# Remaining keys and remaining queries of an attention kernel on four 64x64 tiles of TensorE, in a new order of steps

## The chip, the cores and the metric

The kernel runs on one core of a Trainium2 chip. The metric is the device time of one execution in microseconds (us). Matrix products run on TensorE (PE in the profile; PEld is its loading of weights), the other work on VectorE (DVE), ScalarE (ACT) and GpSimd (POOL); SyncE (SP) issues most DMAs.

## The reference

Attention over 8 batches of 8 heads, 576 positions of 64 channels, with rotary positions on queries and keys, and then a layer of 8 experts of which each token takes its best one.

```python
def rotate(x):
    x1, x2 = (x[..., :half], x[..., half:])
    return np.concatenate([x1 * cos - x2 * sin, x1 * sin + x2 * cos], axis=-1)
q_rot, k_rot = (rotate(q), rotate(k))
scores = scale * np.matmul(q_rot, k_rot.transpose(0, 1, 3, 2))
scores = scores - np.max(scores, axis=-1, keepdims=True)
attn = np.exp(scores)
attn = attn / (np.sum(attn, axis=-1, keepdims=True) + 1e-09)
x = np.matmul(attn, v)            # heads side by side: 4608 tokens x 512
...
expert_idx = np.argmax(x @ w_gate, axis=1)
out = gate_w * (np.maximum(x @ w1[e], 0) @ w2[e])   # e: the token's expert
```

## The kernel before

Attention works on 32 pairs of heads, one pair in a window; the heads of a pair lie on partitions 0 to 63 and 64 to 127. The 576 positions are 512 "main" ones, in four tiles of 128, and 64 "remaining" ones. `PLAN` lists the steps of a window in order, each with its engine (the last letter: p PE, v DVE, a ACT, g POOL, d a DMA on SP's queue) and an offset: window w performs a step with offset -3 for pair w+3. Every engine keeps the order of this list, so an instruction that waits holds up all behind it on its engine. The steps that matter here:

- `FQ`, `FK` load queries and keys, each beside a copy with its two channel halves exchanged. `RQ`, `RK` (L394 to L396) rotate them on POOL: two products and a sum of 128x576 each, into `yq` and `yk`.
- `HQ`, `LQ`, `HK`, `LK` split the rotated values into a high and a low part for fp32r products. `DH`, `DL` are DMAs that copy `q` to the other half of the partitions. `cR` (L438, ACT) copies the remaining queries from `q` into `zq`, which holds zeros between them.
- `S0` to `S8` (L459) are the scores of 128 queries against 576 keys: three products (high by high, low by high, high by low) of 288 columns on each of two row tiles (rows 0 to 63 and 64 to 127), each row tile into a bank of its own. `S4` has the remaining queries of both heads and needs twice as many products, with the zeros of `zq` in the other head's columns. `M` (L470, DVE) takes the scores out of PSUM with their maximum; there are two buffers of scores. `E` (L477, ACT) is the exponential.
- `TA`, `TB`, `TR` (L494, L501, L505) transpose the weights of attention on PE, and `cA`, `cB`, `c1`, `c2`, `c3` (L411) copy them into `PT` (main keys) and `PR` (remaining keys of both heads, 64 partitions each).
- `V0` to `V9` (L534) multiply them with v in fp32, the heads on two column tiles of 64 columns each: five products of 288 columns for each half of the queries, four with main keys and one with the remaining keys, in which `vr` (128x128) holds zeros for the other head. `U` copies the result to `uT`.
- `O` (L555, ten products of 72 columns) turns it to tokens and multiplies with the gate's weights `iw`; `X` (L579, DVE) scales it into `xt`.

The lines named G1 to GS in the plan are places where the steps of the gate are put in: the gate's logits, its choice (`oh`, L143), ranks, stores of tokens, and lists of tokens by indirect DMA from POOL (L694). From the fourth window before the last, the routing (`f1g`, `f1p` and others) comes in small DVE steps behind the steps of `RSTEP`. After the last windows the experts' layer runs over tokens in slots of 256 (L942, L974), its weights split by ACT and DVE (L880, L881); the last pair's `V`, `U`, `O` and `X` are merged with its first products.

A matmul of fp32 data stands in the trace as two matmul instructions, each with its own weight load; one of fp32r as one.

Of the kernel before, what the change touches and what calls it, by code (L numbers as in the profile page):

```python
# [41 lines left out]
STORES = (
    [("gS0d", 3, "GS"), ("gS1d", 4, "GS"), ("gS2d", 5, "GS"), ("gS4d", 5, "ZDd"), ("gS3d", 6, "GS")],
    [("gS0d", 3, "FQd"), ("gS1d", 3, "FKd"), ("gS2d", 3, "DHd"), ("gS3d", 3, "GS"), ("gS4d", 3, "VPd")],
# [33 lines left out]
def kernel(  # L78
# [17 lines left out]
    HS = S // 2  # L96
    XW = D + E
# [338 lines left out]
    def do_cR(st, n):  # L436

        nc.scalar.copy(out=zq[n % 2][:, :, 1:5:2].rearrange("p l a d -> p a l d"), in_=st["q"][:, :, :, 512:576].bitcast(F32))  # L438

    def do_S(st, n, j):  # L440
# [5 lines left out]
        todo = []  # L446
        for hc in (0, 1) if j == 4 else (h,):
            for qp, kp in ((0, 0), (1, 0), (0, 1)):
                todo.append((hc, qp, kp))
        for i_, (hc, qp, kp) in enumerate(todo):  # L450
            for u in range(2):
                r = slice(64 * u, 64 * u + 64)
                other = int(hc != u)
                if j == 4:
                    a = 1 + 2 * other - hc
                    lhs = zq[n % 2][r, qp, a:a + 2].rearrange("p a b -> p (a b)")
                else:
                    lhs = st["q"][r, other, qp, i * P:(i + 1) * P]
                nc.tensor.matmul(sp[:, u, 0:HS], lhsT=lhs, rhs=st["k"][r, kp, hc], start=(i_ == 0), stop=(i_ == len(todo) - 1))  # L459

# [13 lines left out]
    def do_E(st, n, j):  # L474
# [32 lines left out]
    def pt_tiles(st):  # L507
        if "PT" not in st:
            st["PT"] = pp.tile([P, 2, 4, S], F32, name="PT")
            st["PR_"] = pp.tile([P, S], F32, name="PR")  # L510

    def do_c(st, n, h, u, eng):
        pt_tiles(st)
        tp = st.pop(("T", h, u))
        copy(eng, st["PT"][:, h, 2 * u:2 * u + 2, 0:512].rearrange("p k (i b q) -> p b k i q", i=4, b=2),
             tp.rearrange("p b (k i q) -> p b k i q", k=2, i=4))

    def do_c1(st, n, eng):
        pt_tiles(st)
        copy(eng, st["PT"][:, :, :, 512:576], st["TR"][:, :, 0:256].rearrange("p h (k q) -> p h k q", k=4))  # L520

    def do_c2(st, n, eng):
        copy(eng, st["PR_"][:, 0:512].rearrange("p (i b q) -> p b i q", i=4, b=2),
             st["TR"][:, :, 256:512].rearrange("p b (i q) -> p b i q", i=4))

    def do_V(st, n, s):

        half, kt = divmod(s, 5)
        if s == 0:
            st["av"] = tp_tile()  # L530
        hs = slice(half * HS, half * HS + HS)
        for h in range(2):
            r = slice(h * 64, h * 64 + 64)
            nc.tensor.matmul(  # L534
                st["av"][r, half, 0:HS], lhsT=st["vn"][:, h, kt, :] if kt < 4 else vr[n % NVR][:, r],
                rhs=st["PT"][:, h, kt, hs] if kt < 4 else st["PR_"][:, hs], start=(kt == 0), stop=(kt == 4))
# [9 lines left out]
    AHEAD = 2  # L546
    late = []

    def do_O(st, n):

        o = st["O"] = tp_tile()
        for c in range(5 if n >= 0 else 0):
            for h in range(2):
                r = slice(64 * h, 64 * h + 64)
                nc.tensor.matmul(o[:, h, c * XW:c * XW + XW], lhsT=uT[r, c * P:c * P + P], rhs=iw[r, n % NP, :], start=True, stop=True)  # L555
# [633 lines left out]
```

## Time and profile before

| | us |
|---|---|
| median of 3 runs | 965.54 |
| lowest and highest | 962.71, 966.04 |
| the profiled execution, its own time | 964.9 |
| its span, first to last instruction | 963.1 |
| PE busy | 924.5 |
| ACT busy | 678.7 |
| DVE busy | 674.5 |
| POOL busy | 493.8 |

Busy times are means over two stages with different limits: windows of attention up to about 465 us of the span, and the experts' layer behind them.

### The profile page before, as it was taken

How to read it: one execution, taken by the hardware profiler on the slowest of the kernel's cores; microseconds unless marked ns; L12 is line 12 of the kernel's file. 1: busy time of each engine (PE TensorE's matmuls, PEld its weight loads, DVE VectorE, ACT ScalarE, POOL GpSimd, SP SyncE). 2: the span in 40 equal slices, each digit the busy share in tenths (PEclk: the TensorE clock that was granted, in tenths of full speed). 3: DMA queues.
4: the chain of work that ended last, by engine and by line, in shares of the span. 5: the costliest groups of instructions: out<-in, count | busy, mean ns of one | idle time of the engine just before them, and what ended most of it. 6: DMA issues, size and time to landing. Idle time of an engine off the chain costs nothing.

```text
span 963.1 us, 25337 instructions
## 1 busy us (share of the span) xinstructions
PE 924.5 (96%) x9720; PEld 797.8 (83%) x9720; DVE 674.5 (70%) x1354; ACT 678.7 (70%) x1217; POOL 493.8 (51%) x401
## 2 busy tenths in 40 slices
PE   6689999999999999999899999999999999999997
PEld 5578788877788878877698999999999999987886
DVE  5557787878787787886577666666666666667987
ACT  3699999999899999988444455445545545547875
POOL 6888789999899998980424122222222111110111
PEclk7689999999999999999999999999999999999999
DMA  7556666566565666545421377424415311155991
GB/s 256 152 167 186 198 186 204 156 193 196 169 191 159 195 195 190 153 121 156 153 69 47 127 232 234 142 63 153 134 60 184 98 47 47 45 188 190 369 341 51
DMA packets 93139, 153.98 MB, mean 160 GB/s; under 512 B 23127, under 2 KB 56599, under 8 KB 91984
## 3 DMA queue, kind: packets, MB, share of 16 engines
q1 hardware_dynamic: 84720, 129.88, 44.5%
q0 software_dynamic: 8000, 21.20, 6.5%
q8 instruction: 79, 1.29, 0.6%
q10 hardware_dynamic: 288, 1.18, 0.4%
q14 instruction: 52, 0.43, 0.1%
HBM read 162.47 MB, written 23.80 MB: 193 GB/s over the span
## 4 chain that ended last, share of the span: by engine, by line
PE 76%; issue 9%; DMA 5%; POOL 4%; ACT 3%; DVE 2%; another core or an unknown queue 0%; POOLq 0%; SPq 0%; ACTq 0%; DVEq 0%
PE hp L942 18%; PE yp L974 17%; PE tp L534 15%; PE sp L459 13%; PE tp L494 6%; PE tp L555 3%; DMA out_dram<-y,gi 3%; DMA qk<-in_qk_dram 2%; PE xps L897 1%; ACT pn L477 1%; ACT PT L411 1%; PE tp L505 1%; POOL qk L395 1%; PE tp L501 1%; POOL out_dram L984 1%
## 5 line engine op out<-in xcount | busy, mean ns | idle before, releaser
L470 DVE TENSOR_SCALAR_CACHE_REDUCE pn<-sp 128x576 f32<-128x576 f32 x256 | 190.9, 753 | 42.8 <-PE sp L459 39.1
L477 ACT ACTIVATE pn<-pn,negm 128x576 f32<-128x576 f32 x256 | 196.9, 773 | 1.6 <-DVE pn L470 1.6
L459 PE MATMUL sp<-k,q 64*128 64x288 f32 x1536 | 156.3, 322 | 15.9 <-DMA q<-q 8.6
L411 ACT COPY PT<-tp 128x1024 f32<-128x1024 f32 (+1 forms) x160 | 146.1, 929 | 26.7 <-PE tp L494 22.8
L942 PE MATMUL hp<-xh,w1h 128*128 128x256 f32 x544 | 154.3, 284 | 0.7 <-issue 0.4
L942 PE MATMUL hp<-xl,w1h 128*128 128x256 f32 x544 | 154.1, 283 | 0.0
L942 PE MATMUL hp<-xh,w1l 128*128 128x256 f32 x544 | 154.0, 283 | 0.0
L459 PEld LDWEIGHTS sp<-k,q 64*128 64x128 f32 x1536 | 116.0, 195 | 33.8 <-issue 20.8
L984 POOL DMA_INDIRECT out_dram<-y,gi x34 | 34.3, 1008 | 204.4 <-DVE y L147 181.0
L881 DVE TENSOR_TENSOR w2l<-r,w2h 128x1024 fp32r<-128x1024 f32 x92 | 111.6, 1230 | 36.3 <-ACT w2h L880 32.0
L534 PE MATMUL tp<-PT,vn 128*64 128x288 f32 x1024 | 136.7, 409 | 0.0
L974 PE MATMUL yp<-w2h,hh 128*128 128x512 f32 x320 | 126.8, 396 | 0.0
L974 PE MATMUL yp<-w2h,hl 128*128 128x512 f32 x320 | 124.8, 390 | 0.0
L974 PE MATMUL yp<-w2l,hh 128*128 128x512 f32 x320 | 124.6, 389 | 0.0
L881 DVE TENSOR_TENSOR w1l<-r,w1h 128x1024 fp32r<-128x1024 f32 x96 | 113.1, 1218 | 5.4 <-ACT w1h L880 4.4
L534 PEld LDWEIGHTS tp<-PT,vn 128*64 128x64 f32 x1024 | 70.7, 137 | 49.2 <-ACT pn L477 2.6
L942 PEld LDWEIGHTS hp<-xh,w1h 128*128 128x128 f32 x544 | 104.3, 192 | 2.1 <-DVE lpi L140 0.6
L910 ACT ACTIVATE hh<-hp 128x512 fp32r<-128x512 f32 x68 | 40.6, 597 | 91.7 <-PE hp L942 88.4
L942 PEld LDWEIGHTS hp<-xh,w1l 128*128 128x128 f32 x544 | 104.3, 192 | 0.7
L942 PEld LDWEIGHTS hp<-xl,w1h 128*128 128x128 f32 x544 | 104.3, 192 | 0.4 <-issue 0.4
L880 ACT CAST w2h<-r 128x1024 fp32r<-128x1024 f32 x92 | 94.9, 1043 | 11.2 <-PE tp L555 8.3
L880 ACT CAST w1h<-r 128x1024 fp32r<-128x1024 f32 x96 | 95.7, 1051 | 0.0
(194 smaller groups left out, 1805.9 us busy)
## 6 DMA issues: line engine op xcount, KB each, us to landing
r<-in_moe_w_dram SPq DMA_DIRECT2D x192, 512.0 KB
qk<-in_qk_dram SPq DMA_DIRECT2D x64, 576.0 KB
q<-q SPq DMA_DIRECT2D x128, 144.0 KB
x_dram<-xt SPq DMA_DIRECT2D x32, 288.0 KB
vn<-in_v_dram SPq DMA_DIRECT2D x32, 256.0 KB
xlist<-mark SPq DMA_DIRECT2D x8, 289.0 KB
x_dram<-xt SPq DMA_DIRECT2D x8, 144.0 KB
vr<-in_v_dram SPq DMA_DIRECT2D x64, 16.0 KB
```

Source lines behind the costliest of these rows:

```text
L411: (nc.scalar.copy if eng == "a" else nc.vector.tensor_copy)(out=o, in_=i)
L459: nc.tensor.matmul(sp[:, u, 0:HS], lhsT=lhs, rhs=st["k"][r, kp, hc], start=(i_ == 0), stop=(i_ == len(todo) - 1))
L470: nc.vector.tensor_scalar(out=scores(st, n, j), in0=st.pop(("S", j))[:, :, 0:HS], scalar1=-1.0, scalar2=None, op0=ALU.mult, op1=ALU.min, a ...
L477: nc.scalar.activation(out=t, in_=t, func=AF.Exp, bias=st["negm"][:, j:j + 1], scale=-1.0, accum_out=zs[n % 4][:, i, h, 0:1])
L494: nc.tensor.transpose(tp[:, b, c:c + 64], pns[n % 2][r, i, k:k + P], ident[r, r])
L534: nc.tensor.matmul(st["av"][r, half, 0:HS], lhsT=st["vn"][:, h, kt, :] if kt < 4 else vr[n % NVR][:, r], rhs=st["PT"][:, h, kt, hs] if kt ...
L880: nc.scalar.copy(out=hi, in_=src)
L881: nc.vector.tensor_tensor(out=lo, in0=src, in1=hi.bitcast(F32), op=ALU.subtract)
L910: nc.scalar.activation(out=hh, in_=hp, func=AF.Relu)
L942: m = nc.tensor.matmul(hp[:, fi], lhsT=w[:, dc, fs], rhs=x[:, dc], start=(i == 0), stop=(i == len(prods) - 1))
L974: m = nc.tensor.matmul(yp[t], lhsT=h[:, fi, ts_], rhs=w[:, fi], start=(g == 0 and fi == 0 and i == 0), stop=(g == FQ - 1 and fi == 1 and i ...
L984: sc = nc.gpsimd.indirect_dma_start(out=out, out_offset=bass.IndirectOffsetOnAxis(ap=si[:, t:t + 1], axis=0), in_=y, in_offset=None, bound ...
```

## The change

The remaining queries' scores (`S4`) become four fp32 products of 288 columns on four 64x64 tiles: row tile u has head u's bank, column tile hc the head of the queries. They read `yk` itself and a smaller `zq` (128x2x64), filled by `cR`, now a copy on DVE from `yq`, and by two new DMAs (`DR`) that exchange the halves of its partitions. `yk` gets two buffers. `q` holds the 512 main queries alone, so that `HQ`, `LQ`, `DH` and `DL` shrink from 576 to 512 columns.

In the value step each head has a bank and its queries lie in two parts, 256 and 320 columns, on two column tiles; the order of queries in `PT`, `PR`, `uT` and `O` follows. The remaining keys' products of both parts and both heads (`V8`) are four products on 64x64 tiles; two small bf16 products of ones fill the 64 columns that the shorter part leaves. `V9` goes. `U` copies 640 columns instead of 576.

The two products of a rotation become one instruction of 128x1152. `c1` goes from ACT to DVE and `c2` from DVE to ACT. `vr` is 128x64 and loses its zeros, `iw` holds the gate's weights on both sides, the tile of remaining queries takes the third place in `xt` (`CHUNK`), and a store to `x_dram` has runs of two tokens instead of four. The order of the plan, some offsets in it and the places of gate, stores, lists and routing steps are new; the last transposes (`TR`, `TB1`) and `c1`, `c2`, `cB1` move from offset -1 to 0.

```diff
 PLAN = [
...
+    ("TRp", 0), ("S8p", -2), ("c1v", 0), ("TB1p", 0), ("FQd", -4), ("c2a", 0), ("S2p", -2), ("ZDd", 1), ("HQa", -3),
+    ("M8v", -2), ("Op", 2), ("S5p", -2), ("M2v", -2), ("LQg", -3), ("X1v", 2), ("cB1a", 0), ("X0v", 2), ("FKd", -4),
+    ("E4a", -1), ("cRv", -3), ("M5v", -2), ("E2a", -2), ("S1p", -2), ("G1", 0), ("V0p", 1), ("V1p", 1), ("V2p", 1),
+    ("V3p", 1), ("V4p", 1), ("V5p", 1), ("V6p", 1), ("RZv", 1), ("E8a", -2), ("M1v", -2), ("E7a", -1), ("V7p", 1),
+    ("S4p", -2), ("V8p", 1), ("c3v", 2), ("M4v", -2), ("DHd", -3), ("E0a", -1), ("Uv", 1), ("E1a", -1), ("GI", 0),
+    ("E3a", -1), ("HKa", -3), ("DLd", -3), ("RQg", -4), ("S7p", -2), ("GS", 0), ("E6a", -1), ("E5a", -1), ("M7v", -2),
+    ("TA1p", -1), ("S6p", -2), ("LKg", -3), ("cA1a", -1), ("TB0p", -1), ("S3p", -2), ("M6v", -2), ("VPd", -2),
+    ("TA0p", -1), ("M3v", -2), ("G2", 0), ("S0p", -2), ("cB0a", -1), ("cA0a", -1), ("RKg", -4), ("M0v", -2),
+    ("DRd", -3), ("G3", 0),
 ]
...
     for i in range(2):
-        zt = cpool.tile([P, 2, 5, 64], F32R, name=f"zq{i}")
-        nc.vector.memset(zt.bitcast(F32), 0.0)
-        zq.append(zt)
-    uT = pp.tile([P, 640], F32, name="uT", bufs=1)
-    nc.gpsimd.memset(uT[:, S:640], 0.0)
+        zq.append(cpool.tile([P, 2, 64], F32, name=f"zq{i}"))
+    uT = pp.tile([P, 2, 384], F32, name="uT", bufs=1)
+    nc.gpsimd.memset(uT, 0.0)
...
-            nc.sync.dma_start(out=vr[n % NVR][h * 64:h * 64 + 64, h * 64:h * 64 + 64], in_=v[b, h0 + h, 512:576, :])
+            nc.sync.dma_start(out=vr[n % NVR][h * 64:h * 64 + 64, :], in_=v[b, h0 + h, 512:576, :])
...
-    def rotate(n, y, x, cos, sin):
+    def rotate(n, y, x, rot):
         e = V if n == 0 else nc.gpsimd
-        e.tensor_tensor(out=y, in0=x[0], in1=cos, op=ALU.mult)
-        e.tensor_tensor(out=x[1], in0=x[1], in1=sin, op=ALU.mult)
-        e.tensor_tensor(out=y, in0=y, in1=x[1], op=ALU.add)
+        e.tensor_tensor(out=x, in0=x, in1=rot, op=ALU.mult)
+        e.tensor_tensor(out=y, in0=x[:, 0], in1=x[:, 1], op=ALU.add)
...
-        yk = st["yk"] = ld.tile([P, S], F32, name="yk", bufs=1)
+        yk = st["yk"] = rp.tile([P, S], F32, name="yk")
...
-        st["q"] = rp.tile([P, 2, 2, S], F32R, name="q4")
-        copy(eng, st["q"][:, 0, 0], st["yq"])
+        st["q"] = rp.tile([P, 2, 2, SM], F32R, name="q4")
+        copy(eng, st["q"][:, 0, 0], st["yq"][:, 0:SM])
...
-    def do_cR(st, n):
-
-        nc.scalar.copy(out=zq[n % 2][:, :, 1:5:2].rearrange("p l a d -> p a l d"), in_=st["q"][:, :, :, 512:576].bitcast(F32))
+    def do_cR(st, n, eng):
+
+        copy(eng, zq[n % 2][:, 0], st["yq"][:, SM:S])
+
+    def do_DR(st, n):
+
+        z = zq[n % 2]
+        for a in (0, 64):
+            nc.sync.dma_start(out=z[a:a + 64, 1], in_=z[64 - a:128 - a, 0])
...
+        for u in range(2):
+            r = slice(64 * u, 64 * u + 64)
+            if j == 4:
+                for hc in range(2):
+                    nc.tensor.matmul(sp[64 * hc:64 * hc + 64, u, 0:HS], lhsT=zq[n % 2][r, int(hc != u)],
+                                     rhs=st["yk"][r, hc * HS:hc * HS + HS], start=True, stop=True)
+        for i_, (qp, kp) in enumerate(((0, 0), (1, 0), (0, 1)) if j != 4 else ()):
...
     def do_V(st, n, s):
 
-        half, kt = divmod(s, 5)
...
+        for part in (0, 1) if s == 8 else (s // 4,):
+            for h in range(2):
+                a, w = (64 - 64 * h, 256) if part == 0 else (64 * h, 320)
+                x = (320, 0, 0, 256)[2 * part + h]
+                o = st["av"][a:a + 64, h, 0:w]
+                r = slice(h * 64, h * 64 + 64)
+                if s == 8:
+                    nc.tensor.matmul(o, lhsT=vr[n % NVR][r, :], rhs=st["PR_"][r, x + 64 * h:x + 64 * h + w], start=False, stop=True)
+                else:
+                    nc.tensor.matmul(o, lhsT=st["vn"][:, h, s % 4, :], rhs=st["PT"][:, h, s % 4, x:x + w], start=(s % 4 == 0), stop=False)
+        if s == 8:
+            for h in range(2):
+                r, a = slice(h * 64, h * 64 + 64), 64 - h * 64
+                nc.tensor.matmul(st["av"][a:a + 64, h, 256:320], lhsT=onesb[r, 0:64], rhs=onesb[r, 0:64], start=True, stop=True)
 
     def do_U(st, n, eng):
-        copy(eng, uT[:, 0:S].rearrange("p (a b) -> p a b", a=2), st.pop("av")[:, :, 0:HS])
+        copy(eng, uT[:, :, 0:320], st.pop("av")[:, :, 0:320])
...
+        f = o.rearrange("p b s -> p (b s)")
+        todo = ((0, 0, 64), (0, 3, 0), (0, 1, 192), (0, 4, 128), (0, 2, 0), (1, 2, 256), (1, 0, 0), (1, 3, 0), (1, 1, 128), (1, 4, 128))
+        for h, c, x in todo if n >= 0 else ():
+            y = OB + (2 * c + h) * XW
+            r = slice(64 * (y // 512), 64 * (y // 512) + 64)
+            nc.tensor.matmul(f[:, y:y + XW], lhsT=uT[r, h, x:x + P], rhs=iw[r, n % NP, E * h:E * h + XW], start=True, stop=True)
...
```

## Rows read from the trace of the kernel before

**Rows 1.** The page: busy time of PE, and the granted clock in forty slices.

```profile
PE 924.5 (96%) x9720; PEld 797.8 (83%) x9720; DVE 674.5 (70%) x1354; ACT 678.7 (70%) x1217; POOL 493.8 (51%) x401
...
PEclk7689999999999999999999999999999999999999
```

**Rows 2.** Busy time by stretch: us, PE, PEld, DVE, ACT, POOL, granted clock, DMA.

```profile
150.00:200.00 50.00, 50.00 (x758) 40.31 (x756) 38.73 (x108) 47.80 (x101) 46.76 (x37) 1.00 0.67 194
```

**Rows 3.** The chain that ended last, one window: start, us, what.

```profile
113.44 5.00 PE tp L534 x40
...
120.47 0.45 PE sp L459 x6
...
121.42 1.25 PE sp L459 x18
...
123.72 0.85 PE sp L459 x12
...
126.69 0.39 PE tp L534
```

**Rows 4.** Groups of instructions by form, 100 to 400 us.

```profile
L470 DVE TENSOR_SCALAR_CACHE_REDUCE pn<-sp 128x576 f32<-128x576 f32 x178 | 133.1, 753 | 17.9 <-PE sp L459 15.3
...
L534 PE MATMUL tp<-PT,vn 128*64 128x288 f32 x736 | 98.2, 409 | 0.0
...
L395 POOL TENSOR_TENSOR qk<-qk,rotq 128x576 f32<-128x576 f32 x23 | 32.5, 1413 | 0.0
...
L579 DVE TENSOR_TENSOR xt<-tp,rz 128x360 f32<-128x360 f32 x45 | 23.9, 530 | 3.9 <-PE tp L678 2.1 <-PE tp L560 1.0
L459 PE MATMUL sp<-k,zq 64*128 64x288 f32 x264 | 22.9, 306 | 0.0
...
L411 DVE COPY uT<-tp 128x576 f32<-128x576 f32 x22 | 16.7, 758 | 40.8 <-PE tp L534 40.6
...
L411 ACT CAST q<-yq 128x576 fp32r<-128x576 f32 x22 | 14.9, 675 | 0.0
...
L438 ACT CAST zq<-q 128x256 fp32r<-128x256 f32 x22 | 9.0, 409 | 0.0
...
L638 POOL TENSOR_TENSOR dl<-L,mx 128x40 f32<-128x40 f32 x6 | 1.5, 256 | 0.0
```

**Rows 5.** Who waited for whom, 100 to 400 us: total, times, longest.

```profile
DVE uT L411 <- PE tp L534: 40.6, 21, 2.6
POOL yq L394 <- DMA qk<-in_qk_dram: 16.5, 8, 3.1
...
PE tp L494 <- ACT PT L411: 1.1, 3, 0.5
```

**Rows 6.** Matmuls in order of time at the remaining keys' step.

```profile
115.12 0.41 PE L534 MATMUL tp<-PT,vn 128*64 128x288 f32 x2
115.36 0.41 PE L534 MATMUL tp<-PR,vr 128*64 128x288 f32 x2
```

**Rows 7.** The first weight load of a value step, in order of time.

```profile
113.37 0.14 PEld L534 LDWEIGHTS tp<-PT,vn 128*64 128x64 f32 x2 [0.16 <-issue]
```

**Rows 8.** DVE in order of time, around a choice of the gate.

```profile
343.73 1.87 DVE L143 TENSOR_TENSOR oh<-gate_eq,bs 128x40 bf16<-128x40 f32 x1
```

**Rows 9.** POOL in order of time, the same stretch.

```profile
344.11 1.42 POOL L395 TENSOR_TENSOR qk<-qk,rotq 128x576 f32<-128x576 f32 x1
```

**Rows 10.** Durations by tile (least, median, most, ns): `oh`, and the reciprocal `rz`.

```profile
L143 DVE TENSOR_TENSOR oh<-gate_eq,bs x8: 190/1123/1880, 129.5 to 495.9; 128x40 bf16<-128x40 f32 x8
...
L544 DVE RECIPROCAL rz<-rz x32: 216/216/218, 46.8 to 467.8; 128x10 f32<-128x10 f32 x32
```

**Rows 11.** The chain that ended last, start of the kernel.

```profile
31.14 1.40 POOL yk L396
```

**Rows 12.** The chain that ended last, end of attention.

```profile
427.02 1.95 DVE f1p L143
...
460.18 1.99 ACT w1h L880 x2
```

More of the change, by code (lines that the diff above doesn't have):

```diff
@@ L96 @@
     HS = S // 2
+    SM = S - D
     XW = D + E
@@ L363 @@
     for i in range(NVR):
-        t = cpool.tile([P, P], F32, name=f"vr{i}")
-        nc.gpsimd.memset(t, 0.0)
-        vr.append(t)
+        vr.append(cpool.tile([P, D], F32, name=f"vr{i}"))
     def paced(ins):
@@ L445, in do_S @@
         sp = st["S", j] = ps_s.tile([P, 2, 512], F32, name="sp")
[L446 to L450, printed above, removed]
+        for u in range(2):
[5 more added lines that the diff above has]
+        for i_, (qp, kp) in enumerate(((0, 0), (1, 0), (0, 1)) if j != 4 else ()):
             for u in range(2):
                 r = slice(64 * u, 64 * u + 64)
[L453 to L459, printed above, removed]
+                nc.tensor.matmul(sp[:, u, 0:HS], lhsT=st["q"][r, int(h != u), qp, i * P:(i + 1) * P],
+                                 rhs=st["k"][r, kp, h], start=(i_ == 0), stop=(i_ == 2))
     def scores(st, n, j):
@@ L509, in pt_tiles @@
             st["PT"] = pp.tile([P, 2, 4, S], F32, name="PT")
-            st["PR_"] = pp.tile([P, S], F32, name="PR")
+            st["PR_"] = pp.tile([P, S + D], F32, name="PR")
     def do_c(st, n, h, u, eng):
@@ L514, in do_c @@
         tp = st.pop(("T", h, u))
-        copy(eng, st["PT"][:, h, 2 * u:2 * u + 2, 0:512].rearrange("p k (i b q) -> p b k i q", i=4, b=2),
+        copy(eng, st["PT"][:, h, 2 * u:2 * u + 2, 64 - 64 * h:S - 64 * h].rearrange("p k (i b q) -> p b k i q", i=4, b=2),
              tp.rearrange("p b (k i q) -> p b k i q", k=2, i=4))
@@ L519, in do_c1 @@
         pt_tiles(st)
-        copy(eng, st["PT"][:, :, :, 512:576], st["TR"][:, :, 0:256].rearrange("p h (k q) -> p h k q", k=4))
+        t = st["PT"]
+        copy(eng, bass.AP(tensor=t.tensor, offset=t.offset, ap=[t.ap[0], (4 * S + SM, 2), (S, 4), (1, 64)]), st["TR"][:, :, 0:256].rearrange("p h (k q) -> p h k q", k=4))
     def do_c2(st, n, eng):
-        copy(eng, st["PR_"][:, 0:512].rearrange("p (i b q) -> p b i q", i=4, b=2),
+        copy(eng, st["PR_"][:, 64:S].rearrange("p (i b q) -> p b i q", i=4, b=2),
              st["TR"][:, :, 256:512].rearrange("p b (i q) -> p b i q", i=4))
     def do_V(st, n, s):
-        half, kt = divmod(s, 5)
         if s == 0:
             st["av"] = tp_tile()
[L531 to L536, printed above, removed]
+        for part in (0, 1) if s == 8 else (s // 4,):
[12 more added lines that the diff above has]
+                nc.tensor.matmul(st["av"][a:a + 64, h, 256:320], lhsT=onesb[r, 0:64], rhs=onesb[r, 0:64], start=True, stop=True)
     def do_U(st, n, eng):
-        copy(eng, uT[:, 0:S].rearrange("p (a b) -> p a b", a=2), st.pop("av")[:, :, 0:HS])
+        copy(eng, uT[:, :, 0:320], st.pop("av")[:, :, 0:320])
     def do_RZ(st, n):
@@ L546 @@
     AHEAD = 2
+    OB = 512 - 5 * XW
     late = []
@@ L551, in do_O @@
         o = st["O"] = tp_tile()
[L552 to L555, printed above, removed]
+        f = o.rearrange("p b s -> p (b s)")
[4 more added lines that the diff above has]
+            nc.tensor.matmul(f[:, y:y + XW], lhsT=uT[r, h, x:x + P], rhs=iw[r, n % NP, E * h:E * h + XW], start=True, stop=True)
         if n + AHEAD < npair:
@@ L569, in do_c3 @@
                 r = slice(64 * h, 64 * h + 64)
-                copy(eng, state[n + AHEAD]["PR_"][r, 512:576], st["O"][r, h, 5 * XW:5 * XW + 64])
+                copy(eng, state[n + AHEAD]["PR_"][r, S * h:S * h + 64], st["O"][r, h, 360 * h:360 * h + 64])
     def batch(b):
@@ L778 @@
     pns = [np_.tile([P, 4, 2 * S], F32, name=f"pn{i}") for i in range(2)]
-    iw = cpool.tile([P, NP, XW], F32, name="iw")
+    iw = cpool.tile([P, NP, XW + E], F32, name="iw")
     warm = ps_s.tile([P, 2, 512], F32, name="sp")
@@ L789, in setup @@
             nc.scalar.copy(out=t[:, :, E:E + 1], in_=C("bad").unsqueeze(2))
-        for a, g in ((0, 0), (64, D)):
+        for a in (0, 64):
             r = slice(a, a + 64)
-            nc.scalar.copy(out=iw[r, :, E - g // 8:E - g // 8 + D], in_=ident[r, r].unsqueeze(1).broadcast_to([64, NP, D]))
+            nc.scalar.copy(out=iw[r, :, E:E + D], in_=ident[r, r].unsqueeze(1).broadcast_to([64, NP, D]))
     def gate_weights():
-        for a, g in ((0, 0), (64, D)):
-            r = slice(a, a + 64)
-            nc.sync.dma_start(out=iw[r, :, g:g + E], in_=w_gate.rearrange("(r p) e -> p r e", r=NP)[r])
+        for a in (0, 64):
+            for g in (0, D):
+                nc.sync.dma_start(out=iw[a:a + 64, :, g + g // 8:g + g // 8 + E],
+                                  in_=w_gate.rearrange("(r p) e -> p r e", r=NP)[g:g + 64])
     for name in ("RQg", "HQa", "LQv", "DHd", "DLd", "RKg", "HKa", "LKv"):
         step(name, 0, True)
+    for name in ("cRv", "DRd"):
+        step(name, 0, True)
     chained_emit(setup, True)
-    step("cRa", 0, True)
     chained_emit(gate_weights, True)
@@ L815, in rest @@
                     yield
-    WL = npair + max(off for tok, off in PLAN if tok in ("RQg", "RKg", "LQg", "LKg", "HQa", "HKa"))
+    WL = npair + max(off for tok, off in PLAN if tok in ("RQg", "RKg", "LQg", "LKg", "HQa", "HKa", "cRv"))
     WS = npair + max(off for tok, off in PLAN if tok[0] == "S")
@@ L824 @@
     lctx.close()
-    LATE = [f"V{i}" for i in range(10)] + ["U", "O", "X0", "X1", "c3"]
+    LATE = [f"V{i}" for i in range(9)] + ["U", "O", "X0", "X1", "c3"]
     FC = w1.shape[2] // P
@@ L1144, in make_consts @@
     put("upper", (p[:, None] < p[None, :]))
-    tok = np.concatenate([main, (512 + p % 64)[:, None]], 1)
+    tok = np.concatenate([main, (512 + p % 64)[:, None]], 1)[:, [0, 1, 4, 2, 3]]
     valid = np.ones((128, 5))
-    valid[64:, 4] = 0
+    valid[64:, CHUNK[4]] = 0
     put("tid", (np.arange(nb)[None, :, None] * 576 + tok[:, None, :]).reshape(128, nb * 5))
```

50 lines of the change are left out of this document (28 added, 22 removed), and 9 rows, old and new, of the table PLAN.

## The prediction

> **What bounds the kernel now.** I read the page first: PE is busy for 96% of the span, and its granted clock is full (2.4 GHz) from the fourth of forty slices on [rows 1]. The change touches the stage of attention alone. In a table of busy time by stretch PE fills all 50.00 us, ACT 47.80, POOL 46.76, DVE 38.73 [rows 2]: three engines are nearly full, and an edit to PE is worth only as much as the next engine allows. The chain of waits then shows whether PE's busy time is work or waiting: one window runs from the value step at 113.44 to the next at 126.69, 13.25 us, nearly all of it PE's own pieces end to end [rows 3]. In 300 us of such windows the longest of PE's waits for ACT come to 1.1 us, while DVE waits for PE (40.6 us in 21 windows, 1.9 us each) and POOL waits for loads (16.5 us) [rows 5]. PE sets the pace; what PE loses, each window loses, down to the next engine.
>
> Per window of 13.25 us the others carry, from rows 2: ACT 47.80 x 13.25 / 50 = 12.67, POOL 12.39, DVE 10.26.
>
> **Part 1, the value step.** Its 40 matmuls take 5.00 us [rows 3], started in pairs 0.24 us apart, one of each column tile [rows 6]: 20 slots of 288 columns, 0.24 / 288 = 0.83 ns a column. The main keys have 16 slots of 288 columns; afterwards 8 of 256 and 8 of 320, the same columns, so nothing changes there. The remaining keys have 4 slots, 0.97 us. On four tiles all four products run together if tiles that share neither rows nor columns with each other's work are independent: two slots (each fp32 product is two instructions) of 320 columns, 2 x 320 x 0.83 = 0.53 us, a gain of 0.43. If only two run abreast, it is two slots of 256 and two of 320, 0.96 us: no gain. The trace has no 64x64 tile; its nearest rows are column tiles [rows 6] and the scores' row tiles (12 instructions of 288 columns in 0.85 us [rows 3], 0.14 a pair, where one after the other they would need 0.12 each at a column a cycle of 2.4 GHz, 1.44 us). Both kinds pair, so I take the full gain and keep the other end. The two products of ones have 64 columns and start where the shorter part has finished early: 0 to 0.05 us, taken as 0.03.
>
> **Part 2, the remaining queries' scores.** The piece that holds them is 18 matmuls in 1.25 us; the two tiles at 123.72 have 12 in 0.85, so one ordinary tile is 0.42 and these twelve [rows 3, 4] are 0.83 us, six slots. After: four fp32 products of 288 columns, two slots of 0.24 if four abreast, 0.48 us, a gain of 0.35; four slots, 0.96, a loss of 0.13, if two abreast.
>
> **Part 3, PE's order.** The new order puts S4 between V7 and V8, so the four-tile steps stand together, and the array goes from row tiles to column tiles, to four tiles and back: one change more than now. The first weight load of a value step stood 0.16 us on nothing but issue [rows 7]; without a gap it would be 0, and the chain shows no seam behind the step, so I take 0.10. Scores that stand alone take 0.45 to 0.46 where two together take 0.85 [rows 3]; the new order has one such group more: 0.04.
>
> PE per window: -0.43 + 0.03 - 0.35 + 0.10 + 0.04 = -0.61, so 12.64 us. Bounds with four abreast: -0.53 to -0.74.
>
> **Part 4, the cover that the other engines leave.** ACT loses the copy to `zq` (0.41) and 64 of 576 columns of `HQ` (0.675 x 64 / 576 = 0.07) [rows 4]; `c1` and `c2` have 512 columns each and trade places at no cost. ACT has 12.67 - 0.48 = 12.19 of 12.64 us. On POOL a product of 576 columns takes 1.41 us and an operation of 40 columns 0.256 [rows 4]: (1.41 - 0.26) / 536 = 2.15 ns a column and 0.17 fixed. Two merges save 0.17 each at most (0 at least, if the merged one costs twice the row), `LQ` 64 x 2.15 = 0.14: POOL has 11.91 to 12.25. Both stay below 12.64, so none of this is itself worth anything in a full window; it only keeps POOL, at 12.39, from standing too close to the new pace. DVE gains 64 columns of `U` (0.758 for 576 [rows 4], so 0.08) and the new copy, 0.2 to 0.3 by itself.
>
> That copy is the doubtful item. It reads and writes SBUF, as POOL's operations do. The trace shows DVE and POOL collide there: `oh`, with two inputs in SBUF, takes 0.19 us at best but 1.87 at 343.73, and it ended 0.07 behind POOL's product of 344.11 to 345.53 [rows 8 to 10]. The reciprocal, one input and one output in SBUF, takes 0.216 to 0.218 us in all 32 windows, so it never waited [rows 10]. The copy's price lies between 0.22 and a wait like `oh`'s. A merged product lasts 2 x 1.41 - 0.17 = 2.65, and POOL is busy 12.1 of 12.64 us, so a copy that waits for the operation in progress loses, over two of 2.65 and four of about 1.4, (2 x 2.65^2 + 4 x 1.4^2) / (2 x 12.64) = 0.9 us on average and 2.65 at worst. Behind it on DVE are M5 and M1, which free the two score buffers; S4 needs M5's. Ahead of S4 lie V0 to V7, 16 x 0.24 = 3.9 us, in which DVE has two `X`, the copy and M5 to do, 2 x 0.53 + 0.75 [rows 4] and 0.2: cover of 1.9 us. The mean wait is hidden; a wait at its worst, or the mean in the windows that also carry gate steps there (G1), shows. I charge 0.1 us a window, 3 us in all.
>
> The Trainium skill bears on this (page "SBUF — State Buffer", section "SBUF: two separate sides", and "VectorE: DVE Perf Modes", the tier table): DVE and GpSimd share a port pair by an exclusive lock, which a DVE operation needs with two SBUF inputs or in a two-port mode, and an fp32 copy from SBUF to SBUF runs in that mode. `oh` agrees (1.87 against 0.19 us); no row here has such a copy under a running POOL operation. By that rule the copy waits as `oh` does; by the reciprocal's row it doesn't, and the sum would be 3 us less.
>
> The two small DMAs of `DR` join some ten on SP. They stand last on SP in a window, behind `VP`, and S4 asks for them half a window later; the next on SP are loads that wait for their turn anyway. I cost them at nothing; if SP were late, POOL would wait longer for its loads, and it has 16.5 / 22 = 0.7 us a window of that already [rows 5]. The stores' shorter runs and the wider `iw` are likewise off the path.
>
> **Part 5, both ends.** At the start the chain is a load and POOL's rotations up to 32.5 us, nearly two pairs [rows 11]: 0.48 us less for each, -0.8 together. At the end of attention DVE's routing steps collide with POOL (1.95 us for eight numbers) and ACT's weight splits stand ahead of copies that PE waits for (1.99) [rows 12]; with the last transposes a step later these fall elsewhere. I take -1, between +3 and -4.
>
> **Sum.** 32 pairs x 0.61 = 19.5. 964.9 - 19.5 + 3 - 0.8 - 1 = 946.6, against the profiled execution's own 964.9, which is 0.6 below the median of 965.54. I say 947. A change under 0.5% (4.8 us) can't be told from none.
>
> **The rivals.**
> Forecast (chance 0.58): four tiles abreast, PE keeps the pace at about 12.7 us; 947, between 941 and 954.
>
> More than that (0.07): switching costs nothing (-0.71 a window) and the tail gives 4 us: 964.9 - 22.7 - 0.8 - 4 = 937.
>
> Another engine takes the pace (0.18): ACT now stands idle 13.25 - 12.67 = 0.58 us a window; if most of that is order and not slack, the window ends at 12.19 + 0.58 = 12.8 to 13.0, a gain of 0.25 to 0.45. 964.9 - 32 x 0.35 = 954, 950 to 957 with the ends; with POOL's merge worth nothing and a lists' window in which POOL overruns, up to 962. For it: POOL's and ACT's 95% and more. Against: their waits [rows 5] are for PE and for loads, which move with PE. A third of it counts as no change.
>
> Two abreast (0.11), the other side: parts 1 and 2 give 0.0 + 0.13, with 0.17 for parts 3 and the ones: +0.3 us a window, 964.9 + 9.6 - 1.8 = 973. It decides from the point at which the four-tile steps take over 1.6 us instead of 1.02. For it: no 64x64 row. Against: both kinds of pair start together, and the twins of one product do not hold up the other tile's. The skill, "TensorE: Matmul & The Clock Gate", section "Measured speedup vs the span model", has row and column tiles combined at a few ns a tile; no run here shows it yet, and it is the forecast's side.
>
> The copy's wait is not hidden (0.06), also the other side: each window loses 0.9 on DVE and PE with it, net +0.3: 964.9 - 19.5 + 29 - 1.8 = 973; it decides where S4 waits for M5 in every window. For it: `oh`'s row. Against: the reciprocal's, and the 1.9 us. Half of it counts as no change, since part would be hidden. The skill's lock, cited above, speaks for it.
>
> **Chances and range.** Faster: 0.58 + 0.07 + 0.12 = 0.77. The same: 0.06 + 0.03 = 0.09. Slower: 0.11 + 0.03 = 0.14. From 938 to 961 lie the forecast, the second rival and a part of the first: 0.58 + 0.18 + 0.04 = 0.80.
>
> **What the profile will show.** Windows of 12.6 to 12.8 us between value steps; the products of V8 in one piece of about 0.55 us, four starting together, and S4's in about 0.5; PE still with hardly a wait; POOL's products at 2.65 us; the copy on DVE at a mean of about 1 us, with the largest near 2.7. I am wrong if V8 or S4 takes 0.95, if PE waits on `M5` or `M1` in every window, if POOL or ACT shows no idle time, or if attention ends early and the experts' first slot then waits for its weights.

## The result, and the profile after

The changed kernel takes 974.77 us (median of 4 runs, 972.87 to 976.37) against 964.12 for the kernel before on the same chip: ratio 1.0109, 95% interval 1.0075 to 1.0142. It is slower by 1.1%; the prediction, 947 with a range of 938 to 961, said faster by 2%. The profiled execution took 973.34 us with a span of 971.2.

The page of the kernel after, TensorE's row and its granted clock, to be held against [rows 1]:

```profile
PE 923.0 (95%) x9656; PEld 778.2 (80%) x9656; DVE 666.7 (69%) x1382; ACT 665.9 (69%) x1185; POOL 480.0 (49%) x335
...
PEclk7679999999999999999799999999999999999999
```

TensorE's busy time has hardly changed (924.5 before), though its instructions became fewer, and the clock has a dent in the twentieth slice that was not there. Busy time by stretch, after, columns as in [rows 2]:

```profile
150.00:200.00 50.00, 47.52 (x722) 36.44 (x722) 36.52 (x108) 45.00 (x95) 44.03 (x28) 1.00 0.67 183
...
460.00:480.00 20.00, 17.28 (x182) 12.87 (x182) 6.19 (x17) 7.95 (x9) 2.30 (x3) 0.66 0.54 171
```

Where PE filled all 50.00 us, it now stands for 2.48. ACT and POOL lost some 2.8 us each, more than forecast (0.48 us a window in part 4, for POOL at most, which is 1.8 in 50 us). No engine is full any more. One window of PE in order of time (start, us, matmuls; what counts is the time from one start to the next, since the ends are modelled), a window without gate or list work:

```profile
157.73 0.44 PE L542 MATMUL tp<-PT,vn 128*64 128x320 f32 x2
158.10 0.72 PE L454 MATMUL sp<-yk,zq 64*64 64x288 f32 x8
158.63 0.72 PE L540 MATMUL tp<-PR,vr 64*64 64x320 f32 x8
159.07 0.20 PE L546 MATMUL tp<-onesb 64*64 64x64 bf16 x2
159.28 0.66 PE L459 MATMUL sp<-k,q 64*128 64x288 f32 x6
...
162.92 0.42 PE L507 MATMUL tp<-cst,pn 64*128 64x64 f32 x8
163.14 0.66 PE L459 MATMUL sp<-k,q 64*128 64x288 f32 x6
163.62 0.67 PE L496 MATMUL tp<-cst,pn 64*128 64x64 f32 x16
164.09 0.65 PE L459 MATMUL sp<-k,q 64*128 64x288 f32 x6
164.93 1.34 PE L568 MATMUL tp<-iw,uT 64*128 64x72 f32 x20 [0.19 <-ACT PR L409]
```

`S4` (L454) takes 0.53 us from its start to that of `V8`, `V8` (L540) 0.44, the ones (L546) 0.21. That is what the change was to do. Further down, the last score group (164.09) takes 0.84 us to the start of `O` (L568) where the one at 163.14 takes 0.48 to the next piece: `O` waits. Who waited for whom, 100 to 400 us, in the view of [rows 5]:

```profile
DVE rz L145 <- DMA z<-z: 21.7, 20, 1.9
ACT PR L409 <- DVE PT L409: 20.2, 22, 1.3
...
PEld tp L568 <- ACT PR L409: 11.0, 20, 0.8
...
PE tp L568 <- ACT PR L409: 6.3, 19, 0.6
...
PE tp L496 <- ACT pn L478: 5.0, 6, 1.3
...
ACT gate_ex L654 <- POOL dl L651: 4.4, 5, 1.3
```

Before, PE's largest wait for ACT came to 1.1 us over the whole stretch [rows 5]. Now there are three chains that were small or absent. In nearly every window (some 22 lie in the stretch) `c2` on ACT waits for `c1` on VectorE, and `O` for `c2`. In nearly every window VectorE stands before the reciprocal's sum (L145) for `ZD`'s load of `z`: the old plan issues it one window ahead of `RZ`, the new one in the same window. And where a batch's gate falls due, `dl` on POOL holds the exponential on ACT, the exponentials behind it (L478) are late, and PE's transposes (L496) with them.

The first chain by engine, in order of time:

```profile
163.57 0.69 DVE L409 COPY PT<-tp 128x512 f32<-128x512 f32 x1
...
164.29 0.59 ACT L409 COPY PR<-tp 128x512 f32<-128x512 f32 x1 [0.84 <-DVE PT L409]
...
164.93 1.19 PEld L568 LDWEIGHTS tp<-iw,uT 64*128 64x128 f32 x20 [0.42 <-ACT PR L409]
```

`c1` (0.69 us) stands on VectorE behind a maximum of the scores and starts 0.43 after the score group that follows `TR` (163.14); `c2` runs after it and not beside it; both read the PSUM buffer of `TR`, and `O` takes that buffer next (there are two such buffers). The old plan has six pieces of PE between `TR` and the next `O`; the new one has three (`S8`, `TB1`, `S2`), some 1.4 us.

The second chain is hidden in ordinary windows (e5 below), but not in the last ones, where SP is full of stores and weight loads. SP, then VectorE, in order of time:

```profile
454.60 4.07 SPq L671 DMA_DIRECT2D x_dram<-xt  x4
458.91 1.65 SPq L485 DMA_DIRECT2D z<-z  x1
```

```profile
461.25 0.17 DVE L145 TENSOR_REDUCE rz<-z 128x10 f32<-128x20 f32 x1 [6.27 <-DMA z<-z]
...
461.59 0.40 DVE L409 COPY PR<-tp 64x64 f32<-64x64 f32 x2
```

PE in order of time, the same stretch and what follows:

```profile
462.13 1.97 PE L496 MATMUL tp<-cst,pn 64*128 64x64 f32 x32 [3.55 <-DVE PR L409]
...
470.66 6.43 PE L542 MATMUL tp<-PT,vn 128*64 128x256 f32 x32
```

`ZD` (L485) comes late on SP, behind stores of tokens (L671), so VectorE stands for 6.27 us, `c3` behind it is late, and PE stands for 3.55. Then the granted clock falls (0.66 as a mean of 460 to 480 us; its levels are 1.2 and 2.4 GHz), and the value step at 470.66 takes 6.43 us for what takes 4.1 elsewhere.

### The profile page after: what moved, and what is told of

Read it like the earlier page. It is cut to its first block, busy times and chain, and to the rows that moved or that the text cites. A ratio compares the mean times of both kernels' runs of the same rounds, so it can differ in the third digit from the quotient of the medians.

```text
span 971.2 us, 25315 instructions
## 1 busy us (share of the span) xinstructions
PE 923.0 (95%) x9656; PEld 778.2 (80%) x9656; DVE 666.7 (69%) x1382; ACT 665.9 (69%) x1185; POOL 480.0 (49%) x335
## 5 line engine op out<-in xcount | busy, mean ns | idle before, releaser
L471 DVE TENSOR_SCALAR_CACHE_REDUCE pn<-sp 128x576 f32<-128x576 f32 x256 | 186.4, 746 | 34.5 <-PE sp L459 29.8
L478 ACT ACTIVATE pn<-pn,negm 128x576 f32<-128x576 f32 x256 | 195.1, 768 | 2.2 <-DVE pn L471 2.2
L459 PE MATMUL sp<-k,q 64*128 64x288 f32 x1536 | 168.0, 331 | 11.0 <-DMA q<-q 8.9
L459 PEld LDWEIGHTS sp<-k,q 64*128 64x128 f32 x1536 | 118.5, 198 | 26.3 <-issue 17.5
L542 PE MATMUL tp<-PT,vn 128*64 128x320 f32 (+1 forms) x1024 | 134.5, 414 | 0.0
L409 ACT COPY PT<-tp 128x1024 f32<-128x1024 f32 x128 | 125.0, 1013 | 13.5 <-PE tp L496 12.3
L395 POOL TENSOR_TENSOR qk<-qk,rotq 128x1152 f32<-128x1152 f32 x31 | 82.1, 2648 | 45.4 <-DMA qk<-in_qk_dram 42.2
L496 PE MATMUL tp<-cst,pn 64*128 64x64 f32 x2048 | 91.2, 231 | 13.7 <-ACT pn L478 8.5
```

The costliest lines, as they stand in the source:

```text
L395: e.tensor_tensor(out=x, in0=x, in1=rot, op=ALU.mult)
L409: (nc.scalar.copy if eng == "a" else nc.vector.tensor_copy)(out=o, in_=i)
L459: nc.tensor.matmul(sp[:, u, 0:HS], lhsT=st["q"][r, int(h != u), qp, i * P:(i + 1) * P], rhs=st["k"][r, kp, h], start=(i_ == 0), stop=(i_ = ...
L471: nc.vector.tensor_scalar(out=scores(st, n, j), in0=st.pop(("S", j))[:, :, 0:HS], scalar1=-1.0, scalar2=None, op0=ALU.mult, op1=ALU.min, a ...
L478: nc.scalar.activation(out=t, in_=t, func=AF.Exp, bias=st["negm"][:, j:j + 1], scale=-1.0, accum_out=zs[n % 4][:, CHUNK[i], h, 0:1])
L496: nc.tensor.transpose(tp[:, b, c:c + 64], pns[n % 2][r, i, k:k + P], ident[r, r])
```

## The experiments

All times are medians, ratios are to the kernel before on the same chip (963.9 to 964.8 in every set). In the table a span is cut at the starts of the value steps, as read from each trace: up to the first one, the 27 windows from there, the last four, the rest (the experts). Each row is one execution, and executions of one kernel lie 2 to 12 us apart, so a difference of a few us between two rows is only a hint; the length of the ordinary windows, nearly the same all through a trace, is firmer.

```
                     first   27 windows   last 4   rest    span
before                60.7      361.3      52.5    488.6   963.1
after                 61.0      365.3      53.7    491.2   971.2
e1_old_order          63.2      356.1      50.2    492.5   962.0
e2_old_tiles          59.1      388.2      51.7    491.1   990.1
e3_copies_swapped     59.3      360.4      53.6    495.5   968.8
e4b_gate_dve          61.9      367.1      54.9    497.2   981.2
e5_zd_early           60.3      364.6      46.3    491.0   962.2
e8_three_mended       60.4      357.4      47.4    496.4   961.6
e10_copies_zd         61.3      361.8      44.6    491.2   959.0
```

**Tiles or order.** `e1_old_order` has the new tiles and copies with the plan, gate, stores and lists of before (`V9` dropped, `cR` on VectorE behind `RZ`, `DR` last). `e2_old_tiles_new_order` has the old instructions in the new plan (`V9` behind `V8`, `cR` on ACT at the end). The first line of the plan in e1, against after; e2 goes the other way:

```diff
-    ("TRp", 0), ("S8p", -2), ("c1v", 0), ("TB1p", 0), ("FQd", -4), ("c2a", 0), ("S2p", -2), ("ZDd", 1), ("HQa", -3),
+    ("Op", 2), ("FQd", -4), ("M5v", -2), ("S1p", -2), ("G2", 0), ("X0v", 2), ("HQa", -3), ("LQg", -3), ("S7p", -2),
...
```

> The changed kernel with the plan, the gate's places and the routing places of before; S4 stays between TR and S3, V8 follows V7, the copy of remaining queries stands on DVE behind RZ, DR at the end. Theory 'order' (the four-tile steps gain 0.66 us a window as the trace after shows, and the new order gives it back in waits): windows of about 12.5 to 12.6 us, 946 to 950 us in all, two more mode changes included. Rival 'tiles' (the waits come with the new steps and what feeds them, whatever the order): 965 to 976 us, O or the gate still waited for.

> The kernel before (no 64x64 tiles, three rotation operations, fp32r S4 of twelve products) with the plan, gate, stores, lists and routing places of after; V9 behind V8, and the copy to zq on ACT at the end of the window. Theory 'order': it loses about what the order was seen to lose, 0.37 us ahead of O and 0.2 in lone tiles per window, 1.2 us a batch at the gate: 985 to 996 us. Rival 'tiles': 960 to 968 us.

Measured: e1 964.75, ratio 1.0002 (0.9982 to 1.0022); e2 992.54, 1.0292 (1.0261 to 1.0323). The new order costs 28 us with the old tiles and 10 with the new; the new tiles give 18 in the new order, and none that can be measured in the old one. In e1 the attention is 5.2 us shorter over 27 windows, and the last value step comes 5.0 us earlier than before; the start (2.5 later) and the experts (3.9 longer) take nearly all of it back. The waits of e2, 100 to 400 us, show the same chain to `O` as after, and POOL's wait for `HQ`:

```profile
POOL q L422 <- ACT q L414: 29.3, 21, 2.2
ACT PR L414 <- DVE PT L414: 16.4, 20, 2.0
PEld tp L558 <- ACT PR L414: 14.2, 20, 1.8
```

So the loss comes with the order and its copies, not with the tiles.

**`S4` between `V7` and `V8` alone.** `e1b_old_order_s4v8` is e1 with the four-tile steps together (`S4` leaves its place behind `LK`, and `M4` goes behind `M1`):

```diff
-    ("V1p", 1), ("V2p", 1), ("V3p", 1), ("V4p", 1), ("V5p", 1), ("V6p", 1), ("V7p", 1), ("V8p", 1), ("M7v", -2),
+    ("V1p", 1), ("V2p", 1), ("V3p", 1), ("V4p", 1), ("V5p", 1), ("V6p", 1), ("V7p", 1), ("S4p", -2), ("V8p", 1), ("M7v", -2),
...
```

> As e1_old_order, with S4 moved between V7 and V8 and M4 behind M1, so that the four-tile steps stand together. Theory 'order': 3 to 6 us less than e1_old_order if each change of tiling costs 0.1 to 0.2 us, so 942 to 947 us; if a change of tiling costs nothing, the same as e1_old_order. Rival 'tiles': 965 to 976 us.

Measured: 983.53, ratio 1.0202 (1.0172 to 1.0232), a miss. The steps take the 0.54 and 0.44 us of after, but with the scores of `S4` gone from between the transposes, PE waits for ACT's copies in every window:

```profile
PEld tp L493 <- ACT PT L406: 16.4, 21, 0.8
PE tp L493 <- ACT PT L406: 13.6, 21, 0.7
```

In e1, where `S4` stands among the transposes, the change of tiling on both sides of it shows instead: 0.36 us from the transposes in front to `S4` against 0.22 to an ordinary group, and 0.64 for `S4` against 0.54. PE in order of time:

```profile
161.78 0.42 PE L504 MATMUL tp<-cst,pn 64*128 64x64 f32 x8
162.14 0.71 PE L451 MATMUL sp<-yk,zq 64*64 64x288 f32 x8
162.78 0.67 PE L456 MATMUL sp<-k,q 64*128 64x288 f32 x6
```

**The two copies.** `e3_copies_swapped`:

```diff
-("c1v", 0), ("TB1p", 0), ("FQd", -4), ("c2a", 0)
+("c1a", 0), ("TB1p", 0), ("FQd", -4), ("c2v", 0)
```

> The changed kernel with c1 on ACT and c2 on DVE again, nothing else. If O waits for its PSUM buffer until c1 and then c2 have read TR's (one after the other), ACT starts c1 at once where DVE had a maximum to finish, and O's wait of 0.37 us falls to 0.1 to 0.2 us: 965 to 969 us, against 974 to 976 for the changed kernel. If O's wait has another cause: 973 to 977 us.

Measured: 970.98, ratio 1.0059 (1.0035 to 1.0083), a little over what was expected. An ordinary window falls from 13.04 to 12.80 us and 27 windows by 4.9; the experts take 4.3 back in the profiled execution. The windows show the gain clearly; that of the whole run, 3.8 us, is hardly clear of noise, as the intervals of e3 and after overlap a little.

**The load of the sums' row.** `e5_zd_early`:

```diff
-("ZDd", 1)
+("ZDd", 0)
```

> The changed kernel with the load of the sums' row issued in its own window, one window earlier than now. Theory 'order': VectorE's wait for that load, 21.7 us in 20 windows, falls under 3 us, the 3.8 us for which TensorE stands at 458 us goes, and with it the low clock from 460 to 480 us (4.03 us in place of 6.37 us for the value step there): 4 to 8 us, so 967 to 971. Theory 'filled': VectorE is not the engine that the others wait for, the wait costs nothing in the windows, and the tail finds another wait of the same length: 973 to 976.

Measured: 965.92, ratio 1.0008 (0.9979 to 1.0037), 8.9 us less than after and more than expected. The wait leaves VectorE's list, yet the 27 windows gain 0.7 us alone: there it was hidden. The last four gain 7.4, and the stretch that had the low clock (view as above) is whole:

```profile
460.00:480.00 20.00, 18.96 (x200) 12.89 (x200) 12.93 (x24) 10.92 (x14) 8.52 (x8) 1.00 0.47 157
```

**The gate.** `e4_gate_exp_late` puts the exponential later, `e4b_gate_dve` takes the difference in front of it (`dl`) from POOL to VectorE. In e4, and in e6 below, the gate's sum reads the exponentials before they are renewed, so that its weights are not the reference's.

```diff
-("gEa", 2, "E6a")
+("gEa", 2, "cA0a")
```

```diff
-("gDg", 2, "RQg")
+("gDv", 2, "G1")
```

> The changed kernel with one place altered: the gate's exponential on ACT stands after the first copy of the keys' half instead of after the sixth exponential, so that POOL's product in front of it has its time. Theory 'order' (the losses are waits that the new order made, each with its place): the stall of 1.63 us that TensorE shows in one window of each four where the exponential of the gate is due goes, and ACT's waits for that product fall from 4.4 us to under 1.5. Eight times 1.2 is 10 us at most: 963 to 968. Theory 'filled' (TensorE, ACT and POOL are all so full that a wait taken away at one place comes back at the next): the windows keep their sum of 54.3 us in four, 972 to 976.

> The changed kernel with one step altered: the gate's difference from its top score is made on VectorE, right behind the maximum that it needs, instead of on POOL behind the rotation of a pair's queries. The exponential keeps its place on ACT, and finds its input there. Theory 'order': the wait of ACT at the gate's exponential (4.4 us in 5 windows of 100 to 400) and the stall of 1.63 us that TensorE shows behind it go, and up to 1.2 us in eight windows come back: 964 to 970. Theory 'filled': the time comes back at another wait of the same windows, since moving the exponential alone (e4) made its windows longer, 56.6 us in four: 972 to 976.

Measured: e4 979.54, ratio 1.0161 (1.0127 to 1.0194); e4b 979.86, 1.0143 (1.0112 to 1.0175). Neither is faster than after, so "order" fails here; that they are slower isn't clear of noise. In both ACT's wait for `dl` is gone, and the weight loads of `O` wait longer for `c2`, from 100 to 400 us, e4 and then e4b (11.0 after):

```profile
PEld tp L568 <- ACT PR L409: 15.5, 19, 2.1
PEld tp L568 <- ACT PR L409: 15.3, 20, 1.8
```

What was taken out at the gate stood against as much at `O`; that the one made the other is not shown. e4b's experts are also 6.0 us longer.

**Together.** `e6_all_three` has the edits of e3, e5 and e4; `e8_three_mended` those of e3, e5 and e4b; `e11_gate_late_mended` is e6 with the gate's sum and reciprocal at `G3`, behind the exponential; `e10_copies_zd` has e3's and e5's alone.

> The changed kernel with all three: the two copies of the output half traded back between VectorE and ACT, the gate's exponential later, the load of the sums' row earlier. Theory 'order': the gains add, 4 for the copies as measured, up to 10 for the exponential and 4 to 8 for the load: 951 to 959, which is faster than both kernels. Theory 'filled': the attention's loop gets shorter, but the experts' first slot takes it back (it was 3.9 us longer behind the kernel whose loop ended 5.0 us earlier): 960 to 966.

> The changed kernel with the two copies traded back, the load of the sums' row one window earlier, and the gate's difference on VectorE. Theory 'order': the gains of the single edits add, 4 for the copies, 9 for the load and what the gate's edit alone shows (0 to 10): 952 to 962 and faster than before. Theory 'filled': 962 to 966.

> The changed kernel with all three edits, the gate's exponential behind the first copy of the keys' half as in e6 and its sum and reciprocal moved behind it, so that they use the new exponentials (in e4 and e6 they used those of the batch before). Theory 'order': as e6, 958 to 964, and faster than before by 0.2 to 0.6%. Theory 'filled': as e8, 962 to 966, no difference from before.

> The changed kernel with two of the three edits: the two copies traded back and the load of the sums' row one window earlier, the gate as in the changed kernel. Theory 'order': 974.8 less 4 (copies, e3) less 9 (load, e5) is 962, and what this differs from e8 (963.7) is the worth of the gate's edit in that company: 0 to 3 more than e8 if its 2.7 us of shorter windows reach the end, so 963 to 967. Theory 'filled': the shorter loop is taken back at the experts' first products, and the time is that of e8, 961 to 965, whatever the gate does.

Measured: e6 961.48, ratio 0.9965 (0.9942 to 0.9988); e8 963.68, 0.9996 (0.9971 to 1.0020); e11 961.21, 0.9964 (0.9945 to 0.9982); e10 959.21, 0.9930 (0.9911 to 0.9949). e6 and e8 lie where "filled" put them, e11 where "order" did. The two edits without the gate's (e10) beat both kernels, by 0.7% and 1.6%. Neither "order" nor "filled" had that: e10 was expected no earlier than 961. It lies 3 us below what the single gains (3.8 and 8.9) add up to, which the noise of four medians can make. VectorE and PE's loads of e10 at `O`, in order of time:

```profile
162.25 0.69 DVE L409 COPY PR<-tp 128x512 f32<-128x512 f32 x1 [0.34 <-ACT PT L409]
...
163.00 1.19 PEld L568 LDWEIGHTS tp<-iw,uT 64*128 64x128 f32 x20 [0.24 <-DVE PR L409]
```

`O` still waits, but for less. In the profiled execution, its slowest of six, what e10 has over before lies in its last four windows (7.9 us less, where before has one window of 17.1 us); its 27 windows sum to what they did before. An ordinary one is 12.80 for 13.12, and the gate's windows, one of 16.2 us among them, give it back. Its waits, 100 to 400 us:

```profile
ACT gate_ex L654 <- POOL dl L651: 10.3, 6, 2.3
...
PE tp L496 <- ACT pn L478: 6.8, 6, 1.8
```

**The other parts alone.** `e7_three_ops` undoes the merged product, `e9_copy_act` gives the remaining queries' copy back to ACT:

```diff
-        e.tensor_tensor(out=x, in0=x, in1=rot, op=ALU.mult)
-        e.tensor_tensor(out=y, in0=x[:, 0], in1=x[:, 1], op=ALU.add)
+        e.tensor_tensor(out=y, in0=x[:, 0], in1=rot[:, 0], op=ALU.mult)
+        e.tensor_tensor(out=x[:, 1], in0=x[:, 1], in1=rot[:, 1], op=ALU.mult)
+        e.tensor_tensor(out=y, in0=y, in1=x[:, 1], op=ALU.add)
```

```diff
-("cRv", -3)
+("cRa", -3)
```

> The changed kernel with the rotation as three operations of 576 columns again, in place of one of 1152 and one of 576: the merged product undone alone. If the merge is worth nothing because POOL is not what ends the window: 973 to 977. If POOL's time (11.9 to 12.3 us in a window of 13.0) sets the pace together with TensorE, a third operation's start of some 0.1 to 0.3 us in two rotations a window shows: 978 to 985.

> The changed kernel with the copy of the rotated queries' half (L409, one of the two that the change gave to VectorE) on ACT again, at the place that it now has: it can no longer wait for POOL's merged product. If the copy's wait for that product is a cause of the slower time (the rival of the prediction, 0.3 us a window and more): 964 to 969. If it is hidden, as the mean of 277 ns for the copy says: 973 to 977, or more if ACT, which is busy for 45 of 50 us, has no room for it.

Measured: e7 973.01, ratio 1.0085 (1.0058 to 1.0113); e9 976.87, 1.0133 (1.0106 to 1.0161). Both lie where a part that is worth nothing in this kernel would put them. For the merge that is the answer here; e10 without it was not run. e9 alone doesn't clear VectorE's copy, as it also puts work on ACT (its ordinary windows are 13.18 us). The trace after does: `S4`, which a late copy would hold up, starts 4.03 us behind the value step in each of the first 29 windows.

## Why the prediction was wrong

The mechanism of parts 1 and 2 held. Value step and `S4` were to save 0.43 - 0.03 + 0.35 - 0.10 = 0.65 us a window; by their starts they took 5.88 us in an ordinary window before and 4.03 + 0.54 + 0.44 + 0.21 = 5.22 after, 0.66 less. PE before, in order of time:

```profile
140.21 2.16 PE L534 MATMUL tp<-PT,vn 128*64 128x288 f32 x16
142.20 0.66 PE L534 MATMUL tp<-PR,vr 128*64 128x288 f32 x4
142.69 2.11 PE L534 MATMUL tp<-PT,vn 128*64 128x288 f32 x16
144.63 0.66 PE L534 MATMUL tp<-PR,vr 128*64 128x288 f32 x4
145.21 0.67 PE L459 MATMUL sp<-k,q 64*128 64x288 f32 x6
...
148.08 1.04 PE L459 MATMUL sp<-k,zq 64*128 64x288 f32 x12
148.96 0.56 PE L459 MATMUL sp<-k,q 64*128 64x288 f32 x6
```

That the sum is right to 0.01 is luck: the remaining keys went from 1.07 to 0.44 us, 0.63 less where 0.43 was forecast, but the ones (to the next start, the change of tiling included) took 0.21 and the main keys 0.10 more, 3.93 to 4.03, where 0.13 was forecast for ones and changes and nothing for the main keys. The groups by form, after, with counts and mean ns as in [rows 4]:

```profile
L540 PE MATMUL tp<-PR,vr 64*64 64x320 f32 x88 | 15.8, 429 | 0.0
L454 PE MATMUL sp<-yk,zq 64*64 64x288 f32 x176 | 15.7, 428 | 0.0
```

Four run abreast: eight instructions of such a length in 0.44 to 0.54 us. The rivals "Two abreast" and "The copy's wait is not hidden" gave nearly the right time, 973, for the wrong reasons. The section "Measured speedup vs the span model" of the Trainium skill's page "TensorE: Matmul & The Clock Gate", cited against "Two abreast", is borne out by these two rows and by the starts of `S4` and `V8` after.

The step that failed is in part 4, "`c1` and `c2` have 512 columns each and trade places at no cost", with part 3's 0.04 for the order. The durations were right, 0.69 and 0.59 us, but the places were not looked at: the plan puts both between `TR` and an `O` three pieces later. In an ordinary window `O` starts 0.37 us late and is itself 0.10 longer; the score groups take 0.16 more where 0.04 was charged, since six of them now stand alone where three did, not one more; and transposes take 0.05 less: -0.66 + 0.37 + 0.10 + 0.16 - 0.05 = -0.08, as the windows say (13.12 to 13.04). Trading the copies back, alone, returned 0.24 us of that window and some 3.8 us of the run (e3).

Next, `ZD`. Part 4 passed "`DR` ... at nothing" and went on to the queues without holding the offsets of `ZD` and `RZ` against each other: -1 and 0 before, 1 and 1 after. Part 5's "-1, between +3 and -4" for the tail has that size wrong: start, last four windows and rest came out 4.1 us longer, and moving `ZD` alone was worth 8.9 (e5), 7.4 of them in the last four windows.

Third, the sum multiplied one window by 32 (that of [rows 3], 13.25 us; an ordinary one took 13.12). Four windows in a row, those with gate and lists included, took some 53.5 us before and 54.3 after, though two ordinary ones among them were each 0.08 shorter; taking the gate's own wait out did not bring the time back (e4, e4b). The rival "Another engine takes the pace" named such windows, as ones "in which POOL overruns". That e10, at 959, lies in its 950 to 962 doesn't bear it out, since e10 has another plan and its gain is in the last windows. Over all 27 windows 27 x 0.61 = 16.5 us less 2.5 for the copy's wait, 13.9 in all, were forecast as gained, and 4.0 were lost: 17.9 of the 26.7 us between the forecast's -18.3 and the measured +8.4 of the profiled executions (964.9 to 973.34).

POOL's merged product took 2.65 to 2.67 us, as estimated. The copy `cR` was feared too much: a mean of 277 ns in 100 to 400 us against 0.9, and `S4` never late, so the 3 us charged for it were not there. Of the signs listed as making the forecast wrong, PE's waits on `M5` or `M1` and a slow `V8` did not come; TensorE waited on copies, which were not on the list.

What stays open: why the gate's windows got longer, and why the experts take 2.3 to 3.1 us longer than before in every trace of the new plan, with the old tiles too (e2: 491.1). And behind some of these kernels the experts take 3.6 to 6.0 us more than that, or, with the old plan, than before. In these (e1, e1b, e3, e4, e4b, e8) PE stands twice in the first expert products, 1.4 to 1.6 and 2.7 to 3.2 us, and in none of the others. PE in e8, in order of time:

```profile
503.65 0.39 PE L959 MATMUL hp<-xh,w1h 128*128 128x256 f32 x1 [1.50 <-DVE hl L928]
...
509.57 0.39 PE L959 MATMUL hp<-xh,w1h 128*128 128x256 f32 x1 [2.79 <-issue]
```

The longer stand waits for nothing that this profile shows ("issue"); no run tells what makes it, nor whether it comes in every execution of such a kernel.

## What to carry to other kernels

A piece that gets faster on the fullest engine can be worth nothing in a new order. Before it is priced, that order has to be walked through buffer by buffer: for each piece, who frees its buffer, on which engine, behind what, and how many pieces lie between. Compare the offsets of every load with those of its reader in both plans; two that end in the same window are a wait in waiting, hidden as long as the queue is empty. And price the windows that carry extra work apart from the ordinary ones.

## What was not expected of the hardware

A VectorE copy from SBUF to SBUF can wait as `oh` does [rows 8 to 10]. After, in order of time, VectorE and then POOL:

```profile
17.26 2.23 DVE L409 COPY zq<-yq 128x64 f32<-128x64 f32 x1
```

```profile
16.79 2.65 POOL L395 TENSOR_TENSOR qk<-qk,rotk 128x1152 f32<-128x1152 f32 x1
```

A copy whose least time is 0.175 us takes 2.23 and ends at 19.49, 0.05 behind POOL's product (19.44). The lock that the prediction cited (the Trainium skill, "SBUF — State Buffer", "SBUF: two separate sides") agrees with this. That it costs so little in the mean was the surprise. Of the 32 copies only twelve began while POOL had a tensor operation running, and the eight of them that took over 0.35 us ended 0.04 to 0.05 us behind it. Part 4 let the copy fall at any moment of POOL's work. In the fixed plan 28 of the copies began within 1.2 us of the end of `LQ`, with POOL's next product some 0.8 us or more away.

A stand of TensorE can be dearer than itself: behind the one of 3.55 us the value step ran 2.3 us longer, while the clock was low. It need not be. In e9 TensorE stands 4.09 us at the same place, and the value step behind it takes its usual time:

```profile
465.06 1.98 PE L496 MATMUL tp<-cst,pn 64*128 64x64 f32 x32 [4.09 <-DVE PR L409]
...
472.44 4.10 PE L542 MATMUL tp<-PT,vn 128*64 128x256 f32 x32
```

There the granted clock is 0.50 from 465 to 470 us and 0.93 from 470 to 475, where after has 0.50 in both: it was back before the value step began.
